# Attention, norm and MLP in one kernel: from batches in program order to 36 flat 128-token blocks laid out by a list scheduler

## The chip, the cores and the metric

The kernel runs on one core of one Trainium2 chip. The metric is the time of one execution on the device in microseconds, as the median of several executions; lower is better. The engines are called PE or TensorE (matmul), DVE or VectorE, ACT or ScalarE, POOL (GpSimd) and SP (it issues DMAs). Each engine works through its own list of instructions in order.

## The reference

Attention with a window of 128 tokens and a linear distance penalty per head, then a residual block: normalise, multiply by `g`, MLP with ReLU, add.

```python
# q, k, v: (8, 8, 576, 64) float32: batch, head, token, head dimension
scores = q @ k.T / sqrt(64) + slopes[h] * -(i - j)       # 0 <= i - j < 128, else masked
attn   = softmax(scores) @ v                             # -> x: (8, 576, 512)
xn     = (x - mean) / sqrt(var + 1e-6) * g_ln            # over the 512 features
out    = x + relu(xn @ w_ch1) @ w_ch2                    # w_ch1 512x2048, w_ch2 2048x512
```

There are 8 x 576 = 4,608 tokens, that is 36 blocks of 128, or 9 MLP chunks of 512. A batch of 576 tokens is 4.5 blocks.

## The kernel before

Attention goes batch by batch, two heads at a time; the last block of a batch has 64 rows. A Python generator for attention and one for the MLP are advanced in turns, which mixes their instructions; the framework then orders each engine's list further.

```python
def scale_w1():                       # g is folded into w1, on POOL, 16 instructions
    for f0 in range(0, ffn, 512):
        for kb in range(NKB):
            nc.gpsimd.tensor_scalar(out=w1sb[:, kb, f0:f0+512], in0=w1sb[:, kb, f0:f0+512],
                                    scalar1=g_sb[:, kb:kb+1], scalar2=None, op0=ALU.mult)

def attn_gen(b):                      # one batch; yields between steps
    for hp in range(HPAIRS):          # ... cast q and k, transpose, evict ...
        for grp in range(2):
            sc = sc_psum.tile([P, 2, 512], FP32, tag="sc")        # one buffer, two banks
            # ... 4 or 6 score matmuls of 64 rows, in pairs (head g on rows 64*g) ...
            probs = probs_pool.tile([P, 2, 512], FP16, tag=f"pr{grp}")
            nc.scalar.activation(out=probs, in_=sc, func=AF.Exp, scale=inv_sqrt_d)
            # ... VectorE multiplies by the mask ...
        # ... value matmuls (65 columns, the last one gives the row sum), reciprocal, multiply ...
    # whole batch done: bn_stats, bn_aggr; ScalarE: Ln, Exp(-0.5 *) -> rstd
    # ... odd batches: two SBUF-to-SBUF DMAs shift rows by 64 ...
    for tb in range(NSB):
        nc.vector.tensor_scalar(out=xs, in0=xb[:, tb, :], scalar1=mean, scalar2=rstd,
                                op0=ALU.subtract, op1=ALU.mult)
        # ... 4 transposes; ScalarE evicts into xt ...

# mlp_gen(c): 16 groups of 4 matmuls with w1 (ReLU by ScalarE, every 4th by VectorE),
#             then 4 blocks of 16 matmuls with w2; out = pm + x, DMA out

load_w1()
drive(attn_gen(0), None, 0.0)         # batch 0 alone
load_w2()
scale_w1()
for hp in range(HPAIRS):
    load_qkv(1, hp, gates["next"])    # batch 1 is loaded behind the second quarter of w2
for c in range(NCHUNK):               # chunk c of the MLP beside the attention of batch c+1
    drive(attn_gen(c + 1) if c + 1 < B else None, mlp_gen(c), 1.0)
```

PSUM has eight banks: two for scores, two for other attention results, four for the MLP.

The softmax here doesn't subtract the row's maximum and nothing guards it: scores larger than these inputs give would overflow.

## Time and profile before

The time is 389.58 us (389.15 to 389.99). The profiled execution spans 388.6 us.

The first fence is from the kernel before: two rows of its page's table of busy time (engine, busy us, share, instructions), then rows of its 40 equal slices of 9.7 us, each digit the busy share in tenths.

```profile
PE 339.5 (87%) x2528; PEld 166.8 (43%) x2528; DVE 241.3 (62%) x551; ACT 160.9 (41%) x257; POOL 40.5 (10%) x44
...
PE   2443109999999999999999999999999999999996
...
DVE  3443426888777878895878687866676567122221
...
POOL 0640999000000000000000000000000000000000
...
DMA  5799897667774676777657634630010004002002
```

TensorE is mostly idle for six slices and full after that. The windows view of the kernel before shows the same in two stretches (for each engine busy us and, in brackets, instructions; then the granted clock, which is the share of TensorE's full clock that the profile records, the DMA share and GB/s):

```profile
0.00:62.00 62.00, 18.97 (x178) 12.84 (x179) 26.41 (x71) 18.68 (x26) 35.10 (x41) 1.00 0.86 163
62.00:330.00 268.00, 265.72 (x2098) 129.28 (x2097) 203.52 (x465) 127.89 (x207) 5.39 (x4) 1.00 0.50 122
```

In the first 62 us TensorE runs 178 of its 2,528 matmuls. The timeline of the kernel before (start, length, engine, source line, instruction; in square brackets the idle time ahead of it and what ended it) shows the end of that stretch:

```profile
38.27 0.72 POOL L206 CAST vx_124<-v_3_111 128x640 f16<-128x640 f32 x1 [13.74 <-DMA v_3_111<-in_v_dram]
...
41.99 25.40 POOL L162 TENSOR_SCALAR w1sb<-w1sb,g_sb 128x512 f16<-128x512 f16 x16
...
54.77 0.58 DVE L196 CAST s_579<-q_0_100 128x640 f16<-128x640 f32 x1 [10.21 <-DMA q_0_100<-in_q_dram]
...
57.62 1.88 PE L320 MATMUL pxt<-iden,xs 128*128 128x128 f16 x12 [17.43 <-DVE xs L310]
...
61.71 1.91 PE L342 MATMUL pm<-xt_488,w1sb 128*128 128x512 f16 x4
```

Up to 38 us POOL's last v cast of batch 0 has waited 13.7 us for its load. Then between 42 and 61.7 us POOL scales w1. The first MLP matmul starts at 61.71 us.

Steady state: 128 MLP matmuls (one chunk) take 38.06 us, measured from the start of the 257th MLP matmul to that of the 769th, divided by four. The matmuls themselves need 128 x 0.216 = 27.6 us. The remaining 10.4 us belong to one batch of attention, with the waits that it causes.

### The profile page before, as it was taken

The page shows a single profiled execution, that of the slowest core. Times are in us where ns is not written, and L with a number is a line of the kernel's source. Part 1 is how long each engine was busy: PE and PEld are TensorE (multiplying, and loading weights), DVE is VectorE, ACT ScalarE, POOL GpSimd, SP SyncE. Part 2 cuts the span into 40 slices and gives each one's busy share as a digit, 9 for nine tenths or more (in the row PEclk, how much of TensorE's full clock was granted, in tenths as well). Part 3 has the DMA queues.
Part 4 walks back from the last instruction along what each step waited for, and adds up shares of the span by engine and source line. Part 5 has one row for each costly group of instructions (what it writes and reads, how often), then busy time and mean ns, then how long its engine had stood idle before and what let it go on. Part 6 is the DMA issues. An engine that isn't in the chain of part 4 may idle for free.

```text
span 388.6 us, 6535 instructions
## 1 busy us (share of the span) xinstructions
PE 339.5 (87%) x2528; PEld 166.8 (43%) x2528; DVE 241.3 (62%) x551; ACT 160.9 (41%) x257; POOL 40.5 (10%) x44
## 2 busy tenths in 40 slices
PE   2443109999999999999999999999999999999996
PEld 1222104544444455444444444454454444444442
DVE  3443426888777878895878687866676567122221
ACT  3452005632753265426542654366435633511510
POOL 0640999000000000000000000000000000000000
PEclk9999999999999999999999999999999999999999
DMA  5799897667774676777657634630010004002002
GB/s 146 171 174 149 139 198 162 142 146 180 205 160 95 158 180 140 165 185 182 152 132 194 159 90 100 165 88 2 29 54 30 0 29 116 27 27 80 2 27 83
DMA packets 126094, 45.29 MB, mean 117 GB/s; under 512 B 116720, under 2 KB 120816, under 8 KB 126064
## 3 DMA queue, kind: packets, MB, share of 16 engines
q1 hardware_dynamic: 121840, 40.69, 42.6%
q0 software_dynamic: 4224, 4.19, 6.6%
q8 instruction: 20, 0.33, 0.3%
q14 instruction: 10, 0.08, 0.1%
HBM read 37.26 MB, written 9.44 MB: 120 GB/s over the span
## 4 chain that ended last, share of the span: by engine, by line
PE 68%; ACT 11%; DMA 7%; SPq 6%; DVE 4%; issue 2%; POOL 0%; DVEq 0%; POOLq 0%
PE pm L360 29%; PE pm L342 24%; ACT probs L229 8%; PE ptr L199 4%; SPq L97 4%; DMA v_3_111<-in_v_dram 4%; PE sc L221 3%; PE pxt L320 3%; DVE probs L243 3%; PE ppv L255 3%; ACT ht L350 3%; DMA w2sb<-in_moe_w_ch_dram 2%; SPq L103 2%; PE ppv L264 2%; DMA k_0_104<-in_k_dram 1%
## 5 line engine op out<-in xcount | busy, mean ns | idle before, releaser
L360 PE MATMUL pm<-w2sb,ht 128*128 128x512 f16 x576 | 138.8, 379 | 0.0
L350 ACT ACTIVATE ht<-pm 128x512 f16<-128x512 f32 x108 | 64.4, 597 | 75.4 <-PE pm L342 75.4
L229 ACT ACTIVATE probs<-sc 128x1024 f16<-128x1024 f32 x64 | 65.5, 1023 | 57.3 <-PE sc L221 57.2
L360 PEld LDWEIGHTS <-ht 128*128 128x128 f16 x576 | 51.6, 98 | 50.3 <-issue 1.5
L342 PEld LDWEIGHTS <-w1sb 128*128 128x128 f16 x576 | 49.1, 98 | 47.6 <-issue 5.3
L234 DVE TENSOR_TENSOR probs<-probs,mband 128x1024 f16<-128x1024 f16 x32 | 22.4, 701 | 31.8 <-ACT probs L229 29.1
L352 DVE TENSOR_SCALAR ht<-pm 128x512 f16<-128x512 f32 x36 | 24.7, 687 | 27.4 <-PE pm L342 27.2
L255 PEld LDWEIGHTS <-probs 128*128 128x128 f16 x320 | 25.3, 101 | 32.5 <-DVE probs L243 13.1
L203 DVE COPY dst<-ptr 128x640 f16<-128x640 f16 x64 | 31.0, 486 | 11.7 <-PE ptr L199 11.6
L221 PE MATMUL sc<-dst 64*128 64x256 f16 (+2 forms) x320 | 26.9, 265 | 8.1 <-ACT probs L229 4.5
L297 ACT ACTIVATE lv<-mv,eps_t 128x4 f32<-128x4 f32 (+1 forms) x16 | 4.7, 296 | 62.8 <-DVE mv L295 61.9
L243 DVE TENSOR_TENSOR probs<-probs,m2g 128x1024 f16<-128x1024 f16 x32 | 22.3, 695 | 13.6 <-ACT probs L229 12.6
L320 PE MATMUL pxt<-iden,xs 128*128 128x128 f16 x128 | 12.9, 230 | 18.0 <-DVE xs L310 17.9
L221 PEld LDWEIGHTS <-dst 64*128 64x128 f16 x320 | 11.9, 97 | 34.3 <-issue 17.8
L162 POOL TENSOR_SCALAR w1sb<-w1sb,g_sb 128x512 f16<-128x512 f16 x16 | 25.4, 1609 | 0.1
L255 PE MATMUL ppv<-vx_124,probs 128*128 128x65 f16 x160 | 16.3, 206 | 9.1 <-DVE probs L243 4.2
L370 DVE TENSOR_TENSOR o_tile<-pm,xp_3267 128x512 f32<-128x512 f32 x9 | 6.2, 692 | 24.2 <-PE pm L360 24.2
L272 DVE RECIPROCAL rec<-ppv 128x5 f32<-128x5 f32 x64 | 11.6, 191 | 14.3 <-PE ppv L264 13.9
L264 PEld LDWEIGHTS <-probs 128*128 128x128 f16 x256 | 20.5, 102 | 0.1
L320 PEld LDWEIGHTS <-xs 128*128 128x128 f16 x128 | 9.0, 101 | 25.5 <-DVE xs L310 21.3
L342 PE MATMUL pm<-xt_488,w1sb 128*128 128x512 f16 x64 | 17.6, 403 | 0.0
L342 PE MATMUL pm<-xt_520,w1sb 128*128 128x512 f16 x64 | 16.6, 380 | 0.0
(293 smaller groups left out, 410.2 us busy)
## 6 DMA issues: line engine op xcount, KB each, us to landing
out_dram<-o_tile SPq DMA_DIRECT2D x36, 256.0 KB, 2.3
q_0_100<-in_q_dram SPq DMA_DIRECT2D x16, 128.0 KB, 2.6
k_0_104<-in_k_dram SPq DMA_DIRECT2D x16, 128.0 KB, 2.5
v_0_108<-in_v_dram SPq DMA_DIRECT2D x16, 128.0 KB, 2.5
q_1_101<-in_q_dram SPq DMA_DIRECT2D x16, 128.0 KB, 2.6
k_1_105<-in_k_dram SPq DMA_DIRECT2D x16, 128.0 KB, 2.6
v_1_109<-in_v_dram SPq DMA_DIRECT2D x16, 128.0 KB, 2.7
q_2_102<-in_q_dram SPq DMA_DIRECT2D x16, 128.0 KB, 2.6
```

Of the source, the lines that this page charges most:

```text
L162: nc.gpsimd.tensor_scalar(out=w1sb[:, kb, f0 : f0 + 512], in0=w1sb[:, kb, f0 : f0 + 512], scalar1=g_sb[:, kb : kb + 1], scalar2=None, op0= ...
L203: nc.vector.tensor_copy(out=dst[:, :], in_=ptr[:, :])
L221: nc.tensor.matmul(sc[:, g, OFF[j] : OFF[j] + NQ[j]], kt[r0 : r0 + D, j * P : j * P + P], qt[r0 : r0 + D, j * P : j * P + NQ[j]], start=Tr ...
L229: nc.scalar.activation(out=probs[:, :, :], in_=sc[:, :, :], func=AF.Exp, scale=inv_sqrt_d)
L243: nc.vector.tensor_tensor(out=probs[:, :, :], in0=probs[:, :, :], in1=m2g[:, 2 * hp : 2 * hp + 2, :], op=ALU.mult,)
L255: nc.tensor.matmul(ppv[:, qb, :], pr[GRP[qb]][:, g, OFF[qb] : OFF[qb] + P], vx[:, qb, h, 0 : D + 1], start=True, stop=(qb == 0),)
L264: nc.tensor.matmul(ppv[:, qb, :], pr[GRP[j]][:, g, OFF[j] + P : OFF[j] + 2 * P], vx[:, j, h, 0 : D + 1], start=False, stop=True,)
L320: nc.tensor.transpose(pxt[:, kb, :], xs[:, kb * P : kb * P + P], iden[:, :])
L342: nc.tensor.matmul(pm[:, :], w1sb[:, kb, fb * P : fb * P + P], xt[:, kb, :], start=(kb == 0), stop=(kb == NKB - 1),)
L350: nc.scalar.activation(out=ht[:, fb, :], in_=pm[:, :], func=AF.Relu)
L352: nc.vector.tensor_scalar(out=ht[:, fb, :], in0=pm[:, :], scalar1=0.0, scalar2=None, op0=ALU.max)
L360: nc.tensor.matmul(pm[:, :], ht[:, fb, tb * P : tb * P + P], w2sb[:, fb, :], start=(fb == 0), stop=(fb == NFB - 1),)
```

## The change

Intent: make the unit of attention one 128-token block with all eight heads, of which no block is ragged (`where` maps flat blocks to batch and token); start the MLP after four blocks; let a list scheduler in the kernel place every task by assumed durations and priorities; take the scaling of w1 off POOL by multiplying `g` into the normalised rows, and take 1/std out of the way by applying it at the output, where it is a factor per row (ReLU commutes with a positive factor). The essentials of the diff, with arguments shortened:

```diff
+class Plan:   # list scheduler: tasks with engine, assumed time, dependencies, priority, PSUM bank
+    ...       # the order found is emitted as it is, under tc.manual_schedule()
-    sc = sc_psum.tile([P, 2, 512], FP32, tag="sc")
+    sc = psum.tile([P, 4, 512], FP32, tag="sc", name="sc")
+    fb = {n: psum.tile([P, 512], FP32, tag=f"fb{n}", name=f"fb{n}") for n in range(4)}
+    plan.banks["sa"] = [0]
+    plan.banks["sb"] = [1]
...
+    cq = add(f"cq{i}", {"POOL": 0.62}, ...)          # casts of q, k, v: all on POOL
...
+    sa = add(f"Sa{i}", ("PE", 0.38), e_s(0), [ev] + prev, av(i, 2.0), acq=("sa", f"Sa{i}"))
+    sb_ = add(f"Sb{i}", ("PE", 0.38), e_s(1), [sa] + prev, av(i, 2.0), acq=("sb", f"Sb{i}"))
+    # the exponential of half h reads sc[:, 2*h : 2*h+2, :] and frees that half
...
-    scale_w1()
-    nc.vector.tensor_scalar(out=xs, in0=xb, scalar1=mean, scalar2=rstd, subtract, mult)
+    nc.vector.scalar_tensor_tensor(out=xs[i], in0=xb[i], scalar=mean, in1=g_t, subtract, mult)
...
-    nc.vector.tensor_tensor(out=o_tile, in0=pm, in1=x, op=ALU.add)
+    nc.vector.scalar_tensor_tensor(out=ot[i], in0=fb[b], scalar=rstd[c][:, j:j+1], in1=xb[i], mult, add)
...
+    W_AFTER = {0: 4, 1: 8}     # w1 is queued after block 3's loads, w2 after block 7's
```

A block's scores are two groups, `Sa` and `Sb`, of eight 64-row matmuls. The scheduler thinks of them as two resources, `sa` and `sb`, two banks each, so that `Sb` may run while ScalarE still reads `Sa`'s half.

## The prediction

> **What bounds the kernel now.** Two phases. In the 40-slice rows and windows TensorE is mostly idle for the first 61.9 us (18.9 us busy), then 99% busy until 329.6 us, then runs MLP alone. The timeline puts the first MLP matmul at 61.7 us: batch 0 waits for loads (v landed 14.0 us late, behind w1), then POOL scales w1 by g in 16 steps of 1.61 us (25.4 us, from 42.0), and TensorE idles 17.4 us for xs. After that TensorE decides: 1,152 MLP matmuls, 216 ns start to start (the Trainium skill, "TensorE: Matmul & The Clock Gate", § Wait — 56ns, not 53.3ns?, gives 215.7 for 512 columns; the trace agrees), 27.6 us per chunk, 248.6 for nine. Seven chunks share it with a batch of attention at 38.2 us: 10.6 per batch (2.35 per 128 tokens), of which start-to-start times give 8.7 to attention, 1.9 to stretched gaps; the chain passes exponentials again and again.
>
> **What changes.**
> - POOL's w1 scaling goes (25.4 us); g becomes a second tensor of xs on VectorE: 0.41 us to an estimated 0.69, off the path. 1/std leaves the way to the MLP.
> - The first chunk needs 4 blocks; w1 queues after block 3's loads, w2 after block 7's.
> - Full blocks: no SBUF shift copies, no 64-row tails; one DMA of 256 KB instead of three pieces.
> - Casts move from VectorE (0.48, 0.48, 0.81) to POOL (estimate 0.6 each).
> - MLP and attention share four PSUM banks instead of six; scores get four.
> - TensorE per block: 12 transposes at 56-60 ns, 16 score matmuls in row pairs, 16 value matmuls at 30 ns: 1.6 us bare, with switches estimated 1.9. Total 248.6 + 36 x 1.9 = 317 us.
>
> **Sum.** Loads take the 16 DMA engines an estimated 3.7 us per block (from the queue's share), w1 and w2 13 us each. Block 3 lands near 19 us; its chain of short steps and w1's first quarter (10.9 us from issue to landing here) put the first MLP matmul at about 30 us. TensorE's order is fixed: w1 and blocks 4-7 share DMA until about 45, w2 is issued then and lands at 55-62, so the first w2 matmuls stall several us. By 62 us I estimate 35 us of TensorE work done; 282 remain: 344, plus 3.5 for the last output, plus 3-4 of steady stalls: **350 us, 8 in 10 within 337-366**. Faster by over 2%: 0.97; within: 0.02; slower: 0.01. Some 30 of 40 us gained come from the start, 8-10 from steady state.
>
> **Signs.** First MLP matmul 26-36 us; a TensorE gap of 4-10 us before the first w2 matmuls, released by w2's DMA; POOL busy about 70 us, not in the chain after 60 us; TensorE share over 98% from 65 us; middle chunks 35-36 us (for equal work 37 now); VectorE about 215 us; exponentials rarer in the chain.
>
> **What could make it wrong.** (1) The fixed order rests on assumed durations: where POOL's casts run long, TensorE waits in order. The Trainium skill, "SBUF — State Buffer", § SBUF: two separate sides, calls the port pair that VectorE and POOL share an exclusive lock; here a mask multiply took 1.00 us beside POOL copies, 0.69 otherwise. Casts over 1.2 us would make POOL a pacer in the first 60 us. (2) Mask copies on POOL stand before the first v cast (estimate 7 us). (3) Late evictions from four shared banks: each 0.1 us per block is 4 us. (4) Weights landing earlier: 335-340.

## The result, and the profile after

The changed kernel takes 363.14 us (362.82 to 363.5). Its ratio to the kernel before is 0.932, with a 95% interval of 0.9307 to 0.9333. A ratio is the mean time of one kernel's fast runs over that of the other's fast runs of the same rounds, so not quite the ratio of the medians quoted. The profiled execution spans 361.1 us.

The page of the changed kernel, the same rows as above (a slice is 9.0 us here):

```profile
PE 332.4 (92%) x2672; PEld 173.4 (48%) x2672; DVE 216.7 (60%) x444; ACT 157.5 (44%) x237; POOL 78.8 (22%) x127
...
PE   1586999999999999999999999999999999999995
...
DVE  0578497667658666666657666765676667641011
...
POOL 4851541632112121112101211230111100000000
...
DMA  9999999999996444564454346441000010002002
```

Its windows view, with the same first cuts:

```profile
0.00:62.00 62.00, 43.49 (x434) 26.84 (x435) 39.15 (x92) 30.65 (x47) 28.48 (x47) 1.00 1.15 204
62.00:330.00 268.00, 261.57 (x2115) 134.35 (x2113) 173.77 (x348) 117.59 (x176) 50.32 (x80) 1.00 0.45 107
```

At 62 us the changed kernel has done 434 matmuls instead of 178. Of these, 78 are MLP matmuls against 1, worth 77 x 0.216 = 16.6 us; the other 356 against 177 are attention, that is 8.4 blocks (42.2 matmuls each) against 4.6 (38.2 each), worth about 7 us at 1.9 us per block. The lead at 62 us is therefore about 24 us, and the whole gain is 26.4 us: all but two or three microseconds come from the start. Its timeline at the first MLP matmul:

```profile
33.71 0.62 PE L423 MATMUL fb<-vx,probs 128*128 128x65 f16 x8 [0.33 <-DVE probs L409]
34.15 1.90 PE L519 MATMUL fb<-xt,w1sb 128*128 128x512 f16 x4
```

The steady state explains the missing rest. A chunk now takes 36.69 us with four blocks of attention. For equal work the old kernel needed 27.6 + 10.4 x 4 / 4.5 = 36.9 us. So only 0.2 us per chunk was gained there, where the prediction expected one to two (35-36 against 37). TensorE is busy in 97.6% of the middle stretch (261.57 of 268 us), where the old kernel had 99% (265.72). The timeline of the changed kernel shows a gap that recurs:

```profile
145.84 0.23 PE L380 MATMUL sc<-qkt,qkt 64*128 64x128 f16 x2
...
146.17 1.04 PE L545 MATMUL fb<-w2sb,ht 128*128 128x512 f16 x4
146.44 1.02 ACT L403 ACTIVATE probs<-sc 128x1024 f16<-128x1024 f32 x1
...
147.51 0.23 PE L380 MATMUL sc<-qkt,qkt 64*128 64x128 f16 x2 [0.30 <-ACT probs L403]
...
147.95 1.02 ACT L403 ACTIVATE probs<-sc 128x1024 f16<-128x1024 f32 x1 [0.49 <-PE sc L380]
```

Line L380 are the score matmuls. `Sa` of a block starts at 145.84. Four MLP matmuls follow. Then `Sb` of the same block starts at 147.51, just after ScalarE's exponential of `Sa` (146.44 to 147.46) has ended, although it writes other banks. From the start of the last MLP matmul to that of `Sb` it takes 680 ns or 526 ns in such places. Where a score group does not wait, the same step takes 312 ns. From 62 us to the end, the waits view of the changed kernel has only two rows for TensorE. This is the first (who waited, for whom; us in total, times, longest us):

```profile
PE sc L380 <- ACT probs L403: 5.1, 17, 0.3
```

The view understates it, since it counts a modelled end of the matmul before. By start-to-start times, 25 of the 40 steps from an MLP matmul into a score group between 62 and 330 us are longer than 312 ns, by 7.8 us together. The list of instructions shows the same: 36 of the 72 score groups carry a wait on ScalarE, and 32 of these are a `Sb`.

### The profile page after: what moved, and what is told of

Read it like the earlier page. It is cut to its first block, busy times and chain, and to the rows that moved or that the text cites. A ratio compares the mean times of both kernels' runs of the same rounds, so it can differ in the third digit from the quotient of the medians.

```text
span 361.1 us, 6732 instructions
## 1 busy us (share of the span) xinstructions
PE 332.4 (92%) x2672; PEld 173.4 (48%) x2672; DVE 216.7 (60%) x444; ACT 157.5 (44%) x237; POOL 78.8 (22%) x127
## 4 chain that ended last, share of the span: by engine, by line
PE 80%; ACT 12%; DVE 3%; POOL 2%; DMA 1%; issue 1%; SPq 0%; ACTq 0%; DVEq 0%
PE fb L519 32%; PE fb L545 32%; ACT probs L403 8%; PE sc L380 5%; PE fb L423 5%; PE fb L354 4%; PE fb L480 2%; ACT xt L490 2%; ACT ht L531 1%; DMA k<-in_k_dram 1%; DVE probs L409 1%; DVE xb L443 1%; POOL mmix L290 1%; POOL mnew L290 1%; DVE st L459 1%
## 5 line engine op out<-in xcount | busy, mean ns | idle before, releaser
L519 PE MATMUL fb<-xt,w1sb 128*128 128x512 f16 x576 | 140.7, 383 | 0.0
L545 PE MATMUL fb<-w2sb,ht 128*128 128x512 f16 x576 | 137.7, 379 | 0.0
L531 ACT ACTIVATE ht<-fb 128x512 f16<-128x512 f32 x118 | 70.4, 598 | 75.3 <-PE fb L519 75.1
L403 ACT ACTIVATE probs<-sc 128x1024 f16<-128x1024 f32 (+1 forms) x72 | 69.8, 974 | 37.2 <-PE sc L380 36.9
L553 DVE SCALAR_TENSOR_TENSOR ot<-fb,rstd,xb 128x512 f32<-128x512 f32 x36 | 26.8, 748 | 46.4 <-PE fb L545 45.3
L409 DVE TENSOR_TENSOR probs<-probs,mreg 128x1024 f16<-128x1024 f16 (+1 forms) x56 | 37.2, 666 | 24.8 <-ACT probs L403 24.4
L380 PEld LDWEIGHTS <-qkt 64*128 64x128 f16 x544 | 19.4, 98 | 31.8 <-issue 24.7
L423 PE MATMUL fb<-vx,probs 128*128 128x65 f16 x544 | 29.9, 200 | 4.4 <-POOL vx L346 3.1
L380 PE MATMUL sc<-qkt,qkt 64*128 64x128 f16 x256 | 23.0, 229 | 9.4 <-ACT probs L403 6.6
L443 DVE TENSOR_TENSOR xb<-fb,rec 128x256 f16<-128x256 f32 x72 | 30.3, 423 | 2.1
L362 DVE COPY qkt<-fb 128x1024 f16<-128x1024 f16 x36 | 24.7, 686 | 10.4 <-PE fb L354 10.3
L470 DVE SCALAR_TENSOR_TENSOR xs<-xb,mv,g_t 128x512 f16<-128x512 f16 x36 | 28.3, 787 | 1.0
L380 PE MATMUL sc<-qkt 64*128 64x128 f16 x288 | 25.3, 229 | 0.8 <-DVE qkt L362 0.8
```

Of the source, the lines that this page charges most:

```text
L380: nc.tensor.matmul(sc[:, 2 * half + g, c0 : c0 + P], kt[rows, 1, hp, :], qkt[i][rows, 0, hp, :], start=True, stop=True,)
L403: nc.scalar.activation(out=o, in_=n_, func=AF.Exp, scale=inv_sqrt_d)
L409: nc.vector.tensor_tensor(out=pv, in0=pv, in1=mask[:, 2 * half : 2 * half + 2, :, lo:], op=ALU.mult)
L423: nc.tensor.matmul(pp[:, hh * (D + 1) : hh * (D + 1) + D + 1], probs[i][:, bank, slot, side * P : side * P + P], vx[i - 1 + side][:, h, 0 ...
L443: nc.vector.tensor_tensor(out=xb[i][:, 256 * half : 256 * half + 256].rearrange("p (h d) -> p h d", d=D), in0=pp[:, :, 0:D], in1=rec[2 * i ...
L470: nc.vector.scalar_tensor_tensor(out=xs[i][:, :], in0=xb[i][:, :], scalar=mv[c][:, j, 0:1], in1=g_t[:, :], op0=ALU.subtract, op1=ALU.mult,)
```

## The experiments

"Theory 1" is that `Sb` waits because both halves are declared as one tile, so that the framework sees the exponential as a reader of what `Sb` writes. Rivals: switching TensorE between full and 64-row matmuls costs that much (2), or ScalarE is simply late (3).

### Two score tiles

```diff
-    sc = psum.tile([P, 4, 512], FP32, tag="sc", name="sc")
+    sch = [psum.tile([P, 2, 512], FP32, tag=f"sc{n}", name=f"sc{n}") for n in range(2)]
-                                sc[:, 2 * half + g, c0 : c0 + P],
+                                sch[half][:, g, c0 : c0 + P],
```

The two reads in the exponential follow. The traces show the same order of instructions on TensorE, ScalarE, VectorE and POOL as in the changed kernel, one by one.

> The changed kernel with its score PSUM tile declared as two tiles of two banks each; every engine's order of instructions stays as it was, and of the 49 waits on ScalarE in front of score matmuls none is left. Theory 1 (the second score group of a block waits for the exponential of the first group, because both lie in one declared tile): the 680 and 526 ns steps from an MLP matmul into a score group become 312 ns as in the groups that don't wait, about 28 blocks x 0.32 us = 9 us in the dense part and 1-2 us at the start: 352 to 356 us, against 363. Rival 2 (the long steps are the price of going from full-array to 64-row matmuls, whatever the wait): no change, 361-364 us, steps of 680 ns stay. Rival 3 (ScalarE is simply late, the groups wait for a bank truly in use): waits come back in front of the same groups, 360-364 us.

Measured: 353.32 us (352.77 to 353.89), ratio 0.9065 (0.9051 to 0.9078). The same stretch of the timeline, now in the kernel with two tiles:

```profile
123.67 0.23 PE L380 MATMUL sc<-qkt,qkt 64*128 64x128 f16 x2
...
124.00 1.04 PE L519 MATMUL fb<-xt,w1sb 128*128 128x512 f16 x4
...
124.27 1.02 ACT L403 ACTIVATE probs<-sc 128x1024 f16<-128x1024 f32 x1
...
124.97 0.23 PE L380 MATMUL sc<-qkt,qkt 64*128 64x128 f16 x2
```

`Sb` starts at 124.97, 0.32 us before the exponential of `Sa` ends at 125.29. The row of waits on ScalarE is gone; every step from an MLP matmul into a score group is 312 ns; a chunk takes 35.54 us instead of 36.69. TensorE is busy for 199.72 of 200 us from 100 us on, where it was 194.62. The expectation had miscounted the waits: the changed kernel's trace has 36 on ScalarE, not 49, and 6 are left instead of none. Those 6 end no idle time of TensorE in the dense part. Theory 1 is shown, 9.8 us of it, and rivals 2 and 3 fall for the long steps: nothing about the 64-row matmuls or ScalarE's load was changed. Of the 9.8 us, 7.8 are the 25 long steps; 1.9 fell before 62 us, by when this kernel has run 87 MLP matmuls instead of 78 (9 x 0.216), with 356 attention matmuls in both. The clock is no rival: the record has a mean granted clock of 0.981 to 1.0 for these runs and 1.0 for the changed kernel's, and the run at 1.0 took 353.46 us, like the others.

### One run of 16 score matmuls, one tile

```diff
-        sa = add(f"Sa{i}", ("PE", 0.38), e_s(0), [ev] + prev, av(i, 2.0), acq=("sa", f"Sa{i}"))
-        sb_ = add(f"Sb{i}", ("PE", 0.38), e_s(1), [sa] + prev, av(i, 2.0), acq=("sb", f"Sb{i}"))
+        sa = sb_ = add(f"S{i}", ("PE", 0.76), e_s2, [ev] + prev + last_ex, av(i, 2.0))   # both halves
```

> The changed kernel with the one score tile kept, but both score groups of a block issued as one run of 16 matmuls (the schedule is computed anew with that). Theory 1: no exponential of the same block stands between them, so the wait of 0.2-0.37 us goes here too (-9 us), and one switch into and out of 64-row matmuls per block goes with it (96 + 120 ns x 28 = -6 us): 346 to 352 us. Rival 2 (all of the 680 ns is switching): half of all switches gone, 345-350 us; so this run alone doesn't tell 1 from 2, e1 does. Rival 3: 360-364 us.

Measured: 348.1 us (347.38 to 349.01), ratio 0.8932 (0.8915 to 0.8949), a chunk in 34.59 us. That is 5.2 us less than with two tiles. The wait is absent here for another reason: no exponential of the block stands between its halves. And one change into 64-row matmuls and one back fall away per block. In the trace of the two-tile kernel the change in costs 96 ns over the plain step (312 instead of 216), the change back 92 ns (148 from the last score matmul to the next matmul, against 56 on average from one pair of score matmuls to the next; the expectation's 120 took the average over single matmuls). Some 28 fewer of each in the dense part make an estimated 5.3 us, close to the 5.2 measured. The schedule was computed anew, so the order of TensorE's list differs as well, and this split is an estimate. So rival 2 named a real cost, 96 of the 408 ns by which the long steps exceed a plain one on average, but not the cause of the rest.

### Both mends together

> Both mends together: two score tiles and one run of 16 score matmuls. Theory 1: with one run per block there is no wait left in the dense part that a second tile could take away, so the same time as one run on one tile: 346-350 us; the start, where blocks follow each other closely, may gain up to 1.5 us. Rival 3 (true lateness of ScalarE): the same. So a gain over 2 us would show that waits on the shared tile were left in the one-run kernel.

Measured: 347.98 us (347.35 to 348.38), ratio 0.8916 (0.8891 to 0.8942), chunk again 34.59 us. As expected, with one run per block the second tile has nothing left to do.

### Mask copies later on POOL

```diff
-        vv = av(3, 0.0) - 200
+        vv = av(3, 0.0)          # and the three memsets' priorities likewise
```

> The changed kernel with POOL's copies for the two special masks moved behind casts in its queue, so that the first v cast comes at about 7.5 us instead of 12.2. If the start hangs on that (chain of waits: mask copies, v cast, first value matmuls, VectorE in order): first MLP matmul at 31-32 us instead of 34.3, 359-361 us in all. If the start hangs on the loads of blocks 3 and 4 and w1: first MLP matmul stays at 33.5-34.5 us and the time at 362-364.

Measured: 364.21 us (363.81 to 365.68); the first MLP matmul at 35.8 us instead of 34.2. The first value matmuls did start earlier, at 11.5 instead of 12.9 us, but nothing came of it. The first branch of the expectation is refuted; the second missed as well, by 1.3 us at the first MLP matmul and 0.2 us in all. The mask copies, risk (2) of the prediction, do not set the start alone; that the loads do is not shown by this run.

### The kernel before without the scaling of w1

```diff
-    scale_w1()
```

Its output is wrong, which doesn't matter for the time.

> The kernel before without the scaling of w1 by g on POOL (a wrong result on purpose). If POOL's 25.4 us of scaling holds the first MLP matmul back, as the prediction said: first MLP matmul at 45-52 us instead of 61.7, 374-382 us. If the start hangs on the load order (batch 1's q is loaded only behind w2, and VectorE's cast of it stands before the tail's statistics and xs): first MLP matmul at 59-61.7 us, 387-390 us.

Measured: 387.82 us (387.05 to 388.23) against 389.8 of the same rounds, ratio 0.9953 (0.9937 to 0.997); first MLP matmul at 59.4 us. The 25.4 us of POOL's work were worth 2 us in the old kernel. The prediction's reading of the old start, with the scaling as one of its links, was wrong in this.

### g back on w1, in the changed kernel

```diff
-            nc.vector.scalar_tensor_tensor(out=xs, in0=xb, scalar=mean, in1=g_t, subtract, mult)
+            nc.vector.tensor_scalar(out=xs, in0=xb, scalar1=mean, scalar2=None, op0=ALU.subtract)
+    # 16 POOL tasks tensor_scalar(w1sb, g) after w1's landing; each w1 group depends on its quarter's
```

> The changed kernel with g put back: POOL scales w1 in 16 steps after it has landed, xs only subtracts the mean (tensor_scalar), all else as changed. If g's place matters in the new plan (POOL now also has all casts in its in-order queue, so 25.7 us of scaling stands in front of the casts of blocks 5 to 8): first MLP matmul at 37-42 us, 370-378 us against 363. If the scaling is as well hidden as it was in the kernel before (2 us there): 362-366 us.

Measured: 374.46 us (373.48 to 375.03), ratio 0.9595 (0.9566 to 0.9624), 11.3 us more than the changed kernel. The first MLP matmul came at 33.3 us, as early as without it, so that number of the expectation missed; the loss comes later. POOL's timeline in this run:

```profile
29.93 19.10 POOL L323 TENSOR_SCALAR w1sb<-w1sb,g_t 128x512 f16<-128x512 f16 x12
48.97 3.04 POOL L328 DMA_DIRECT2D w2sb<-in_moe_w_ch_dram  x4
52.01 4.68 POOL L323 TENSOR_SCALAR w1sb<-w1sb,g_t 128x512 f16<-128x512 f16 x3
56.62 0.63 POOL L346 CAST q<-q 128x512 f16<-128x512 f32 x1
```

The next q cast waits behind the scaling until 56.6 us, and TensorE lacks attention work: by 62 us it has run 212 attention matmuls instead of 356. The issue of w2's DMA stands behind the scaling too: POOL comes to it at 48.97 us instead of 44.11. In the waits view of this run from 45 to 70 us these are the two longest rows for TensorE's matmuls (us in total, times, longest us); the changed kernel has neither:

```profile
PE fb L554 <- DMA w2sb<-in_moe_w_ch_dram: 4.6, 1, 4.6
PE fb L528 <- POOL w1sb L323: 2.3, 2, 1.1
```

After the wait for w2, MLP matmuls step at 427 ns instead of 216 until 60.2 us, which costs another 2.1 us. So g's place is worth 2 us in the old kernel and 11 us in the new one, because in the new one POOL's list also holds every cast, and w2's DMA behind the scaling. How the 11 us divide among the casts, w2 and the scaled w1 was not separated.

### The old norm whole, in the changed kernel

As above, and Ln, Exp per block ahead of `xs`, which again multiplies by 1/std; a plain add at the output.

> As the run before this one, and 1/std back in xs too (ln and exp per block on ScalarE ahead of xs, a plain add at the output): only the flat blocks and the list scheduler are left of the change. If 1/std is off the path in steady state: 0 to 3 us over the run with g on w1 alone (ScalarE gets about 14 us more work, and each of the first blocks 0.5 us more latency): 370-381 us. If ScalarE's longer queue delays the exponentials that the score groups wait for: 5 us or more over it.

Measured: 375.97 us (375.61 to 377.21), ratio 0.9642 (0.9612 to 0.9672): 1.5 us over the run before it, with a chunk in 36.83 us. Moving 1/std to the output is worth little (tried only with g on w1). Flat blocks and scheduler alone, still with the shared score tile, are 14 us better than the kernel before.

### The kernel before with batch 1's loads not held behind w2

```diff
-        load_qkv(1, hp, gates["next"])
+        load_qkv(1, hp, gates["w1"])
```

> The kernel before, right in its result, with one change: batch 1's loads no longer wait until a part of w2 has landed (they may go as soon as their buffers are free). Load-order theory (VectorE's casts of batch 1 stand before the tail's last statistics and xs of batch 0 in its queue, and wait for loads that were held behind w2; that, not POOL's scaling, kept the first MLP matmul at 61.7 us): first MLP matmul at 49-56 us, 378-384 us. Scaling theory (POOL's scaling from 42 to 67 us holds the start): first MLP matmul stays at 60-62 us, 387-391 us.

Measured: 393.15 us (391.72 to 394.2), ratio 1.0074 (1.004 to 1.0108), first MLP matmul at 63.7 us. Both expectations missed. The framework moved still more of batch 1's casts ahead of batch 0's statistics; in the timeline VectorE idles 8.7 us for q of batch 1's first pair and 5.6 us for its second pair at 54.2 us. Earlier issue did not bring the data earlier beside w1 and w2. The run settles nothing about the order itself, hence the next one.

### The kernel before with batch 0's norm first

```diff
+    # VectorE's casts of batch 1 depend on the last xs of batch 0
+    # chunk 0's 16 w1 groups come before batch 1's attention; ScalarE takes all its ReLUs
```

> The kernel before, right in its result, with orders changed only: VectorE's casts of batch 1 come after batch 0's last xs, the 16 w1 groups of chunk 0 come before batch 1's attention on TensorE, and ScalarE takes all of chunk 0's evictions; loads and POOL's scaling stay. If it was the in-order casts that held the first MLP matmul at 61.7 us: it comes at 47-50 us (v landed near 38, statistics, xs, first scaled quarter of w1 at 48.4). The total then shows whether the new start is kept: 378-384 us if so; 386-392 us if chunk 1, which needs the whole of batch 1, gives it back. If POOL's scaling or the loads themselves held it: still 58 us or later.

Measured: 403.03 us (400.49 to 404.39), ratio 1.0318 (1.0278 to 1.0357). The first MLP matmul came at 49.5 us, as expected if the in-order casts had held it; the total got 13 us worse, beyond both ranges given. TensorE's timeline in this run:

```profile
49.48 9.06 PE L347 MATMUL pm<-xt,w1sb 128*128 128x512 f16 x34
59.66 0.39 PE L347 MATMUL pm<-xt,w1sb 128*128 128x512 f16 x1 [1.12 <-POOL w1sb L162]
61.44 3.47 PE L347 MATMUL pm<-xt,w1sb 128*128 128x512 f16 x15 [1.40 <-POOL w1sb L162]
66.06 0.39 PE L347 MATMUL pm<-xt,w1sb 128*128 128x512 f16 x1 [1.15 <-POOL w1sb L162]
```

Started early, the MLP does run into POOL's scaling. And chunk 1 needs most of batch 1's attention, which now had less MLP work beside it to fill TensorE's waits: from 100 to 120 us TensorE is busy for 10.6 us, at a granted clock of 0.57, where the kernel before had 19.8 us at 1.00. An early first MLP matmul is worth nothing in itself: what counts is how much of TensorE's work is done by then and can go on. That the changed kernel can go on because its next chunk needs four blocks, not a batch, is the likely reason; no run shows it alone.

### Weights one block earlier, and measured durations

Both have the two mends. The first has `W_AFTER = {0: 3, 1: 7}`; the second has the scheduler's assumed durations replaced by traced ones (for instance 0.64 us instead of 0.76 for the score run).

> Two score tiles, one score run per block, and w1 queued after block 2's loads and w2 after block 6's (one block earlier). If w1's landing sets the first MLP matmul: 2-3 us earlier than 34.1, 345-346 us. If block 3's and 4's own loads and chain set it: they now share DMA with w1 from earlier on, first MLP matmul at 34-37 us, 347-351 us. I expect the second.

> Two score tiles, one score run per block, and the scheduler's table of durations set to what the trace shows (transposes 0.45, a score run 0.64, value matmuls 0.24, xs transposes 0.23, xs and output op 0.75 us). If assumed durations cost time through a wrong fixed order: 1-4 us less than 348. If they were near enough, and the engines' in-order queues absorb the rest: 346.5-349.5 us. I expect the second.

Measured: 348.54 us (348.21 to 349.78), first MLP matmul at 35.8; and 347.79 us (347.09 to 348.32), first MLP matmul at 35.0, ratio 0.8908 (0.8884 to 0.8932). Neither differs by more than the noise from 348.0. An earlier place of w1 in the queue does not bring the start forward, and the assumed durations were near enough.

## Why the prediction was right or wrong

The measured 363.14 us lies in the range of 337 to 366, 3 us from its far end, and "faster" came true. The middle, 350, was 13 us too low, and what moved it was none of the named risks. That it was faster was no luck: the start alone, with 24 us, carries it.

- **Steady stalls, "3-4 of steady stalls", and "8-10 from steady state": wrong.** This is the step that failed. The scheduler's two score resources were taken at their word; that both halves were one declared tile was not weighed. The waits on the shared tile, above all that of `Sb` for the exponential of `Sa`, cost 9.8 us (353.32 against 363.14) where 3-4 us of stalls were allowed for, and a chunk took 36.69 us where 35-36 was predicted. With the wait gone it takes 35.54, inside the predicted range. The named risk, (3) late evictions from the four shared banks, was not it: between consecutive MLP matmuls the excess over 216 ns adds up to 0.3 us from 100 to 300 us. Two signs of the prediction had missed and pointed here: TensorE's share was 97.6% instead of over 98%, and the exponentials were no rarer in the chain of work that ended last (8.4% of the span, 8.1% before).
- **TensorE's own cost of attention: nearly right.** 1.9 us per block was predicted. Start-to-start times between 100 and 300 us of the attention matmuls sum to 40.2 us for 922 of them, 21.8 blocks, so 1.85 per block with the ways back from 64-row pairs in it. The 30 ways in from an MLP matmul, at 96 ns, add 0.13. The chunk of 35.54 us without the wait gives the same, (35.54 - 27.65) / 4 = 1.97.
- **The start: about right in size, partly wrong in cause.** First MLP matmul at 34.15 us, predicted about 30 and within 26-36. TensorE's work done by 62 us is 78 x 0.216 + 356 / 42 x 1.9 = 33 us, predicted 35; the kernel with two score tiles, with 87 MLP matmuls, reaches 34.8, so what was missing is again the wait. The predicted gap of 4-10 us before the first w2 matmuls did not occur: w2 was issued at 44.1 us and landed in a median of 11 us, but TensorE, slower through chunk 0 than assumed, asked for it only at 57.0.
- **POOL's scaling as the bound of the old start: wrong** (2 us there). Removing it was worth 11 us, but in the new plan, through the casts and w2's DMA behind it. The prediction had not seen this coupling.
- **Off the path, as predicted:** VectorE 216.7 us (about 215); xs at 0.75 us (0.69); POOL 78.8 us (about 70), with casts at 0.62 (0.6). The Trainium skill, "SBUF — State Buffer", § SBUF: two separate sides, has VectorE, with some of its instructions, and POOL lock each other out of a shared port pair; here single instructions show such lengthening (a mask multiply up to 1.02 us against a median of 0.68, a cast up to 1.11 against 0.62), each while the other engine was busy, but the medians are undisturbed, and no wait of TensorE after 62 us comes from POOL.
- **The tail** took 4 us from the last matmul to the end of the span, predicted 3.5; and the time is 2 us over the span.

In the prediction's own terms the sum closes to within 2 us: 344 + 3.5 for the last output, + 9.8 for the wait in place of the 3-4 of stalls, + about 2 for attention at 1.97 instead of 1.9 us per block, + about 2 for the time over the span, makes 361. The start needs no term of its own, since its shortfall is part of the 9.8.

Still open: what sets the first MLP matmul of the new kernel at 33 to 36 us. Mask copies, w1's place and assumed durations were each changed without moving it forward. The loads are an obvious suspect, with a DMA share of 1.15 up to 62 us, but the chain view of the changed kernel (work that ended last, followed back; start, length, what) has none between 5.9 us and the first MLP matmul:

```profile
1.69 4.15 DMA k<-in_k_dram
...
5.89 0.62 POOL k L337
6.50 1.97 POOL mmix L290 x2
...
12.26 0.57 POOL vx L346
...
33.71 0.62 PE fb L423 x8
34.34 1.71 PE fb L519 x4
```

In between stand scores and exponentials in turn (15.7 to 21.5 us) and then VectorE, almost without a break, from 22.1 to 30.7. With the masks later the chain goes another way, again without a load after 7.2 us; with the weights one block earlier it goes through a v load from 14.2 to 29.0. So it looks as if several chains of about the same length lie side by side; no run shortened more than one of them. Nor does a run show what it costs that TensorE steps at half its later rate at first (transposes at 107 ns, the first MLP step of 216 ns only at 37.8 us). How the 14 us of flat blocks and scheduler divide between the two was not separated either.

## What to carry to other kernels

A scheduler's resources and the framework's tiles must be the same things: if two halves of a tile are to be used independently, declare two tiles, and look in the instruction list for waits that the plan does not know of. Judge a shorter start by the work the busiest engine has finished at a fixed time, not by when its first main instruction begins, and value a saving on one engine in the plan it will live in: the same 25 us on POOL were worth 2 us in one and 11 in the other. Among equals, group the matmuls of one shape: one run of 16 score matmuls instead of two of 8 saved another 5 us, and 347.8 to 348.1 us is the best measured here.

## What the Trainium skill lacked or had wrong

- "TensorE: Matmul & The Clock Gate", § Back-to-back issue gap, says a real stream of weight load and matmul sustains about 81 ns per matmul at 128 columns and 131 at 512. These runs show 56 ns (transposes, each with its own weight load) and 216 ns in long runs of such pairs; its formula for the isolated gap fits, the sustained figures do not.
- The same page, § Part 4: PE-mode transpose, says that the full clock does not engage for transposes. Here transposes that stand among other matmuls step at 56 ns once TensorE is busy, and at 107 ns in the first 34 us; both match the warm and cold gaps of its Part 1. No run here has transposes alone. In these first microseconds the profile's clock row prints full clock, but 107 ns is what the steps show.
- No page gives a time for changing between full matmuls and pairs of 64-row matmuls in one stream: 96 ns on the way in and 92 ns on the way out over the plain steps. "TensorEngine Tiling (Array Packing)", § Key Properties, has only that a change of tiling mode drains TensorE. "TensorE: Matmul & The Clock Gate", § Part 3, gives about 4 ns between the starts within a pack; after 62 us pairs here start 3 to 19 ns apart in the changed kernel and 3 to 5 in the one with two tiles.
- "PSUM — Partial Sum Buffer", § PSUM bank collisions raise a hardware error, says to guard PSUM by bank and quadrant, or simply by bank. It does not warn that a wider declared tile makes the guard wider: here that was 9.8 us of 363.
